# A state-space scan with an ELU layer on one core: block 0's and block 1's C loaded as squares by head pair, and the last four row pieces multiplied tile by tile

## The chip, the cores and the metric

The kernel runs on one core of one Trainium2 chip. The metric is device time in microseconds of one execution, lower is better. A core has a matrix engine (TensorE, PE in the profile, with its weight loads as PEld), a vector engine (VectorE, DVE), an engine for functions (ScalarE, ACT), a general engine (GpSimd, POOL) and one that here only issues transfers (SyncE, SP). Each works through its own queue in program order; semaphores join them. Transfers run on 16 DMA engines.

## The reference, cut to what matters

```python
# x: (4, 8, 768, 32), a: (4, 8, 768), B and C: (4, 8, 768, 16)
for c in range(24):                       # chunks of 32 tokens
    cum = cumsum(log(clip(a_c)))
    M = (C_c @ B_c.T) * exp(cum_i - cum_j) * causal
    y_c = M @ x_c + (C_c @ state) * exp(cum)
    state = exp(sum) * state + sum_j(B_j x_j * exp(cum_last - cum_j))
h = y.reshape(3072, 256) @ w_in           # heads side by side; w_in: 256 x 2048
g = where(h > 0, h, exp(min(h, 0)) - 1)
out = g @ w_out                           # w_out: 2048 x 256
```

The two weight matrices arrive as 64-bit floats; the kernel reads them as pairs of 32-bit words and makes float32 of them itself.

## The kernel before, in words

**Blocks.** The 3072 rows are worked on in 12 blocks of 256 tokens (`place`, L103, gives batch and group). Each block is first scanned, with inner chunks of 64 tokens, and its result, transposed, goes through the two weight matrices. There are no loops on the chip: the Python loops write out one long program, and the order in it is the order on each engine.

**The scan of a block.** B and C of a block lie in one tile `bc`, with tokens on the 128 partitions. `load_bc` (L121) loads B and C for both halves (`u`) of 128 tokens, in runs of 16 numbers, 64 bytes. For blocks from 4 on, and for C of block 1, `load_squares` (L111) loads the same data in another order, runs of 8 tokens by 16 numbers, so that 32 by 32 squares can be transposed by VectorE (`turn_square`, L454). The plain form is transposed by TensorE: `turn` (L430) transposes B and C, copies B from PSUM on ScalarE (`bt`) and makes on VectorE the C that is masked by head (`ctm`, L444); `turn_b` (L420) does B alone; `mask_heads` (L466) makes `ctm` from a square. `scaled` (L410) multiplies B by its decay, `turn_exp` (L448) multiplies C by the decay from the chunk's start (`cts`). Then `sums` (B times x), `states` (the running state, VectorE, and its masked copy, GpSimd), `scores` (C times B), `weigh` (L558, the scores times the decays, VectorE), `across` and `inside` (the carried and the inner part of y, TensorE), and copies into `yT`. For blocks 0 and 1 the decays come from a short first load of `a` (four loads of 32 rows, L93); `la` (L259) is the whole of `a`, clipped (L1118), turned into logarithms (L1154), and summed for all later blocks, whose sums go through memory (`write_flat`, `spread_cum`).

**The weights.** `w_load(i)` (L173) loads piece i of w_in (512 KB, piece 0 in two parts). Each piece is made into float32 by a fixed series: magnitude on ScalarE (`w_abs`, L201), low word on ScalarE or VectorE (`w_low`), sign and two steps on VectorE (`w_sign`, `w_high_a` L239, `w_high_b` L246), and the sum on GpSimd (`w_sum`, L256), for pieces 2 and 3 in two halves. Then `l1` (L678) multiplies.

**The start of the program.** All loads but two go out on SyncE's queue, in this order: two of the four `a` loads, B of block 0 (two halves), `la`, x of block 0 (two), piece 0 (two parts), piece 1, C of block 1 as two square loads, B's first half of block 1, piece 2, B's second half, piece 3, x of block 1 with piece 4 between its halves. ScalarE's queue carries the other two `a` loads and C of block 0 (two halves). The part that follows (from L1114) interleaves block 0's scan, pieces 0 to 3 and block 1's scan by hand; there `scaled(1)` (L1169, GpSimd) stands ahead of the sum of piece 2.

**The end of the program.** The last two blocks' second multiplication (`second_words`, L1029) is done in split words: each row piece m of 16 (`TURN`, L1009, the last 14 of them) has three products for each of the four tiles t of 128 rows: kind 1 into `both`, kinds 0 and 2 into `high[t]`. A loop does all products of a piece, four tiles by three kinds, and with them makes the words of the piece six places on (`high_of_g`, `rest_of_g` L1022). The last two pieces are done apart: first kind 1 for all tiles, whose result ScalarE scales into `e` (L1074), then kinds 0 and 2 tile by tile. After tile 1 VectorE combines tiles 0 and 1 (L1081), after tiles 2 and 3 each of those, and each tile is stored by a transfer of 128 KB, in turn on ScalarE's and SyncE's queue.

Of the kernel before, what the change touches and what calls it, by code (L numbers as in the profile page):

```python
# [32 lines left out]
def kernel(  # L33
# [69 lines left out]
    def place(n):  # L103

        return 2 * (n // (2 * NG)) + n % 2, n // 2 % NG
# [5 lines left out]
    def load_squares(n, k):  # L111
        b, g = place(n)
        squares = st[n]["bc"].rearrange("p k u h n -> p k (u h n)").rearrange(
            "p k (m r) -> p k m r", m=2)
        for m in range(2):
            nc.sync.dma_start(
                out=squares[:, k, m],
                in_=(B, C)[k][b, m:NH:2, g * BLK:(g + 1) * BLK, :].rearrange(
                    "q (c t) n -> q c (t n)", t=8))

    def load_bc(n, c_queue=nc.sync, us=(0, 1)):  # L121
        b, g = place(n)
        if "bc" not in st.setdefault(n, {}):
            st[n]["bc"] = raw.tile([P, 2, 2, NH, N], F32, tag="bc", name="bc", bufs=2)
        if n > 3:
            for k in range(2):
                load_squares(n, k)
            return
        for u in us:
            sl = slice((2 * g + u) * P, (2 * g + u + 1) * P)  # L130
            for k, src in enumerate((B,) if n == 1 else (B, C)):
                (nc.sync, c_queue)[k].dma_start(
                    out=st[n]["bc"][:, k, u], in_=src[b, :, sl, :].rearrange("h s n -> s h n"))

    def load_b(n):
# [37 lines left out]
    def w_load(i, parts=1):  # L173
        if i < len(pieces):
            w_raw[i] = conv.tile(
                [P, parts, 2, 2 * CW // parts], U32, tag="s64" if 5 <= i < 8 else "w64", name="w64",
                bufs=3 if 5 <= i < 8 else W_AHEAD - 3)
            for part in range(parts):
                cols = slice(2 * CW * part // parts, 2 * CW * (part + 1) // parts)
                nc.sync.dma_start(out=w_raw[i][:, part], in_=pieces[i][1][:, :, cols])  # L180
# [74 lines left out]
        w = pieces[i][0].bitcast(U32)[:, ks, cols]  # L255
        nc.gpsimd.tensor_tensor(out=w, in0=w_mag[i][:, ks, cols], in1=w, op=ALU.add)  # L256

    load_bc(0, nc.scalar)
    nc.sync.dma_start(out=la, in_=a.rearrange("b h (g c s) -> (b h g) c s", g=NG, s=P))  # L259
    load_x(0)  # L260
    w_load(0, 2)

# [167 lines left out]
    def turn(n):  # L430

        s = st[n]
        tb, tc_ = psum([P, 2, P], "ps_tb"), psum([P, 2, P], "ps_tc")
        for k, ps in enumerate((tb, tc_)):
            for u in range(2):
                nc.tensor.transpose(
                    out=ps[:, u], in_=s["bc"][:, k, u].rearrange("p h n -> p (h n)"),
                    identity=ident)
        s["squares"] = att.tile([P, 2, 2, P], F32, tag="bct", name="bct", bufs=2)
        s["bt"] = s["squares"][:, 0]  # L440
        nc.scalar.copy(out=s["bt"], in_=tb)
        s["ct"] = tc_
        s["ctm"] = att.tile([P, 2, 2, P], F32, tag="ctm", name="ctm")
        nc.vector.tensor_tensor(  # L444
            out=s["ctm"], in0=tc_.unsqueeze(2).to_broadcast([P, 2, 2, P]),
            in1=hmask2.unsqueeze(1).unsqueeze(3).to_broadcast([P, 2, 2, P]), op=ALU.mult)
# [19 lines left out]
    def mask_heads(n):  # L466
        s = st[n]
        s["ctm"] = att.tile([P, 2, 2, P], F32, tag="ctm", name="ctm")
        for us, eng in ((slice(0, 1), nc.vector), (slice(1, 2), nc.gpsimd)) if n == 1 else (
                (slice(0, 2), nc.vector),):  # L470
            count = us.stop - us.start
            eng.tensor_tensor(
                out=s["ctm"][:, us], in0=s["ct"][:, us].unsqueeze(2).to_broadcast([P, count, 2, P]),
                in1=hmask2.unsqueeze(1).unsqueeze(3).to_broadcast([P, count, 2, P]), op=ALU.mult)
# [354 lines left out]
    def row_of(n):  # L829
        b, g = place(n)  # L830
        return b * S + g * BLK
# [197 lines left out]
    def second_words(n):  # L1029

        both = [psum([P, 2, DM], "ps_w") for _ in range(2)]
        high = psum([P, 2, DM], "ps_o")
        high = [high[:, 0], high[:, 1], psum([P, DM], "ps_o"),
                p_o.tile([P, DM], F32, tag="o", name="ps_o")]

        def product(m, t, kind):
            lhs = h_of[m][kind][:, t // 2, t % 2 * P:(t % 2 + 1) * P]
            nc.tensor.matmul(  # L1038
                out=both[t // 2][:, t % 2] if kind == 1 else high[t], lhsT=lhs,
                rhs=out_words(m // 2, kind, m), start=(m == TURN[0] and kind == 0 and t != 1),  # L1040
                stop=(m == TURN[-1] and kind > 0), skip_group_check=True)

        store(n - 2, 0)
        store(n - 2, 1)
        given_back(slice(1, 4))
        for m in range(2):
            for t in range(4):
                nc.tensor.matmul(  # L1048
                    out=both[t // 2][:, t % 2], lhsT=g_of[n, m][:, t // 2, t % 2 * P:(t % 2 + 1) * P],
                    rhs=scaled_rows[0][:, m], start=(m == 0 and t % 2 == 0), stop=False,  # L1050
                    skip_group_check=True)
        rest_of_g(n, TURN[4])
        high_of_g(n, TURN[5])
        rest_of_g(n, TURN[5])
        for at, m in enumerate(TURN[:-2]):
            if at + 6 < len(TURN):
                high_of_g(n, TURN[at + 6])
            if at == 0:
                end_words()
            if at + 6 < len(TURN):  # L1060
                rest_of_g(n, TURN[at + 6])
            if at in (0, 2, 4):
                high_of_out(4 + at // 2)
            if at in (1, 3, 5):
                rest_of_out(4 + at // 2)
            for t in range(4):
                for kind in (1, 0, 2):
                    product(m, t, kind)
        e = [ffn.tile([P, 2, DM], F32, tag="e", name="e", bufs=2) for _ in range(2)]
        for b in range(2):  # L1070
            for t in (2 * b, 2 * b + 1):
                for m in TURN[-2:]:
                    product(m, t, 1)
            nc.scalar.activation(e[b], both[b], ACT.Copy, scale=WORD)  # L1074
        for t in range(4):
            for m in TURN[-2:]:
                product(m, t, 0)
                product(m, t, 2)
            for to in ((), (0, 1), (2,), (3,))[t]:
                o = e[to // 2][:, to % 2]  # L1080
                nc.vector.scalar_tensor_tensor(  # L1081
                    out=o, in0=high[to], scalar=WORD - 1.0, in1=o, op0=ALU.mult, op1=ALU.add)
                r0 = row_of(n + to // 2) + to % 2 * P
                (nc.scalar if to % 2 == 0 else nc.sync).dma_start(out=out[r0:r0 + P, :], in_=o)

    def store(n, at):
        r0 = row_of(n + at)
# [15 lines left out]


    w_load(1)
    load_bc(1, us=())
    load_squares(1, 1)
    load_bc(1, us=(0,))
    w_load(2)
    load_bc(1, us=(1,))  # L1110
    w_load(3)
    load_x(1, 4)
    half = [slice(0, P), slice(P, 2 * P)]
    first_low(0)  # L1114
    first_cum(0)
    first_decays(0, 0, 1)
    eb0 = turned(E0, "eb0", 1.0, nc.vector)
    clip(la)  # L1118
    turn(0)
    first_decays(0, 2)  # L1120
    first_exp(0)
    first_decays(0, 3)
    scaled(0, nc.gpsimd)
    turn_exp(0)
    sums(0, parts=(most,))
    states(0, most)
    w_abs(0, half[0])
# [17 lines left out]
    w_high_b(0, half[1])  # L1145
    kept = st[0]
    inside(y, 0)
    w_low(0, nc.scalar, half[1])
    w_sum(0, half[1])
    first_low(1, p_o)  # L1150
# [377 lines left out]
```

## Time and profile before

| what | value |
|---|---|
| time, median of 3 runs | 347.93 us (346.98 to 347.99) |
| profiled execution | 347.17 us, its span 345.5 us |
| TensorE busy | 337.1 us (98%), 3836 products |
| VectorE busy | 272.6 us (79%) |
| ScalarE busy | 250.1 us (72%) |
| GpSimd busy | 209.7 us (61%) |
| granted TensorE clock | 1.000 |
| TensorE idle, 15.95 to 27.23 us | 11.28 less 9.70 busy |
| TensorE idle, 27.23 to 341.00 us | 313.77 less 313.50 busy |
| DMA | 28.57 MB in 76645 packets, 57848 of them under 512 B |
| DMA engines busy, 5 to 25 us | nearly all the time, 221 to 262 GB/s |

The profile is of one execution. A line of a timeline gives the start in us from the start of the span, the length, the engine and the line of the code, the operation, what it writes and from what, and in brackets how long its engine stood idle before it and whom it waited for. A line with x2 or more merges instructions that follow one another. In the chain of waits each line is the piece of work that released the next; SPq and ACTq are the queues' own instructions, such as the issue of a transfer. "Busy" of TensorE says that it has products under way, not that it could do no more.

### The profile page before, as it was taken

What the parts mean: (1) busy time and instruction counts of PE and PEld (TensorE: products, weight loads), DVE (VectorE), ACT (ScalarE), POOL (GpSimd) and SP (SyncE); (2) the same over time, 40 slices, a digit from 0 to 9 for tenths busy, and PEclk for the clock granted to TensorE, in tenths of its full rate; (3) what the DMA queues carried; (4) which work ended last, traced back from release to release, by engine and by line L of the source; (5) the groups of instructions that cost most, each with busy time, mean ns of one, the idle gap of its engine ahead of it and who ended that gap; (6) DMA issues with size and microseconds to landing.
All of it is one profiled execution on the core that took longest, in us unless ns stands there. A gap on an engine that the chain in (4) does not pass through costs nothing.

```text
span 345.5 us, 9778 instructions
## 1 busy us (share of the span) xinstructions
PE 337.1 (98%) x3836; PEld 295.2 (85%) x3836; DVE 272.6 (79%) x527; ACT 250.1 (72%) x565; POOL 209.7 (61%) x303
## 2 busy tenths in 40 slices
PE   8889999999999999999999999999999999999994
PEld 5668888888788898889899888999988999999994
DVE  4898888879898778866788666879776778887991
ACT  5789889599759898657699457699557567768511
POOL 5754553559988799964396764296754562753600
PEclk9999999999999999999999999999999999999999
DMA  8988998380796961160421160510000100001001
GB/s 144 239 214 194 309 192 214 77 156 31 110 153 107 143 105 29 18 155 2 109 61 31 17 153 5 121 17 3 2 0 4 64 0 3 0 0 61 2 2 62
DMA packets 76645, 28.57 MB, mean 83 GB/s; under 512 B 57848, under 2 KB 71480, under 8 KB 76600
## 3 DMA queue, kind: packets, MB, share of 16 engines
q1 hardware_dynamic: 69960, 25.40, 32.1%
q0 software_dynamic: 4176, 2.10, 5.5%
q10 hardware_dynamic: 2464, 0.46, 0.7%
q8 instruction: 30, 0.49, 0.6%
q14 instruction: 15, 0.12, 0.1%
HBM read 22.51 MB, written 3.34 MB: 75 GB/s over the span
## 4 chain that ended last, share of the span: by engine, by line
PE 90%; DVE 3%; SPq 2%; DMA 2%; issue 1%; ACT 0%; DVEq 0%; ACTq 0%
PE ps_o L905 29%; PE ps_h L798 19%; PE ps_h L678 10%; PE ps_w L798 10%; PE ps_o L842 8%; PE ps_o L1038 4%; PE ps_y L645 2%; PE ps_w L1038 2%; DMA w<-in_moe_w_in_dram 2%; PE ps_g L552 2%; PE ps_y L627 1%; PE ps_st L582 1%; PE ps_w L1048 1%; SPq L180 1%; DVE g L700 1%
## 5 line engine op out<-in xcount | busy, mean ns | idle before, releaser
L815 ACT ACTIVATE e<-ps_h 128x512 f32<-128x512 f32 x72 | 43.1, 598 | 48.2 <-DVE ps_h L809 48.1
L823 DVE SCALAR_TENSOR_TENSOR g<-e,ps_h 128x512 f32<-128x512 f32 x72 | 49.3, 684 | 29.4 <-ACT e L816 29.0
L905 PEld LDWEIGHTS ps_o<-w_out,g 128*128 128x128 f32 x512 | 64.0, 191 | 3.4
L905 PE MATMUL ps_o<-w_out,g 128*128 128x128 f32 x512 | 65.3, 275 | 0.0
L809 DVE SCALAR_TENSOR_TENSOR ps_h<-ps_h,e 128x512 f32<-128x512 f32 x72 | 50.0, 694 | 11.5 <-ACT e L806 10.7
L798 PE MATMUL ps_w<-y_both,w_words 128*128 128x512 f32 x144 | 51.1, 435 | 0.0
L806 ACT ACTIVATE e<-ps_w 128x512 f32<-128x512 f32 x72 | 42.1, 584 | 10.8 <-PE ps_w L798 10.7
L678 PE MATMUL ps_h<-yT,w_in 128*128 128x256 f32 (+1 forms) x208 | 45.4, 368 | 2.5 <-POOL w_in L256 0.6
L816 ACT ACTIVATE e<-e 128x512 f32<-128x512 f32 x72 | 45.5, 632 | 2.3
L798 PE MATMUL ps_h<-y,w_words 128*128 128x512 f32 x144 | 46.0, 401 | 0.0
L798 PE MATMUL ps_h<-y,w 128*128 128x512 f32 x144 | 44.7, 392 | 0.0
L858 POOL TENSOR_TENSOR g<-g 128x256 f32<-128x256 f32 x28 | 22.2, 794 | 36.4 <-DVE g L823 36.2
L678 PEld LDWEIGHTS ps_h<-yT,w_in 128*128 128x128 f32 x208 | 36.2, 190 | 8.5 <-POOL w_in L256 3.4
L532 ACT ACTIVATE L<-L,ncum 128x64 f32<-128x64 f32 x160 | 42.2, 336 | 0.4 <-DVE ncum L377 0.4
L537 POOL TENSOR_SCALAR_AFFINE_SELECT L<-L 64x512 f32<-64x512 f32 x40 | 30.0, 750 | 9.0 <-ACT L L532 7.6
L798 PEld LDWEIGHTS ps_h<-y,w 128*128 128x128 f32 x144 | 27.0, 188 | 6.5 <-POOL w L858 0.2
L905 PE MATMUL ps_o<-w_sum,g 128*128 128x128 f32 x256 | 32.6, 275 | 0.0
L905 PEld LDWEIGHTS ps_o<-w_sum,g 128*128 128x128 f32 x256 | 31.4, 192 | 1.3 <-ACT c_sum L942 0.3
L798 PEld LDWEIGHTS ps_h<-y,w_words 128*128 128x128 f32 x144 | 26.4, 188 | 5.7 <-issue 0.4
L842 PE MATMUL ps_o<-w_out,g 128*128 128x256 f32 x128 | 31.0, 384 | 0.0
L842 PEld LDWEIGHTS ps_o<-w_out,g 128*128 128x128 f32 x128 | 23.7, 190 | 4.0 <-ACT ob L848 0.4
L858 POOL TENSOR_TENSOR g<-t,g 128x256 f32<-128x256 f32 x32 | 23.0, 747 | 5.8 <-PE ps_o L905 5.7
(144 smaller groups left out, 636.9 us busy)
## 6 DMA issues: line engine op xcount, KB each, us to landing
L<-flat SPq DMA_DIRECT2D x20, 256.0 KB
w<-in_moe_w_out_dram SPq DMA_DIRECT2D x8, 512.0 KB
w<-in_moe_w_in_dram SPq DMA_DIRECT2D x7, 512.0 KB
xr<-in_x_dram SPq DMA_DIRECT2D x24, 128.0 KB
out_dram<-c_sum SPq DMA_DIRECT2D x8, 256.0 KB
bc<-in_B_dram SPq DMA_DIRECT2D x24, 64.0 KB
w_sum<-w_out POOLq DMA_DIRECT2D x3, 512.0 KB, 8.9
bc<-in_C_dram SPq DMA_DIRECT2D x22, 64.0 KB
```

Source lines behind the costliest of these rows:

```text
L532: nc.scalar.activation(L[:, h, u], L[:, h, u], ACT.Exp, bias=ncum[:, u, row:row + 1])
L537: nc.gpsimd.affine_select(out=part, in_=part, pattern=[[0, 4], [0, 2], [1, Q]], compare_op=ALU.is_ge, fill=0.0, base=0, channel_multiplier=-1)
L678: nc.tensor.matmul(out=ps[:, j, toks], lhsT=w_in[i][:, k, j * P:(j + 1) * P], rhs=yT[n // 2][:, k, n % 2].rearrange("p u i -> p (u i)")[:, ...
L798: nc.tensor.matmul(out=ps, lhsT=lhs[:, k], rhs=rhs[:, k], start=k == 0 and lhs is not w0, stop=k == KC - 1 and lhs is not w1)
L806: nc.scalar.activation(e, both, ACT.Copy, scale=WORD)
L809: nc.vector.scalar_tensor_tensor(out=high, in0=high, scalar=WORD - 1.0, in1=e, op0=ALU.mult, op1=ALU.add)
L815: nc.scalar.activation(e, high, ACT.Relu, scale=-1.0)
L816: nc.scalar.activation(e, e, ACT.Exp, scale=-1.0)
L823: nc.vector.scalar_tensor_tensor(out=g_of[n, m].rearrange("p b i -> p (b i)"), in0=e, scalar=1.0, in1=h, op0=ALU.subtract, op1=ALU.max)
L842: nc.tensor.matmul(out=o_of[n][:, ts], lhsT=g_of[n, j][:, m % 2, ts * P:(ts + 1) * P], rhs=w_out[:, m], start=(m == 0 and ts == 0), stop=( ...
L858: nc.gpsimd.tensor_tensor(out=out, in0=in0, in1=in1, op=ALU.subtract)
L905: nc.tensor.matmul(out=ps[:, ts], lhsT=b[:, ts * P:(ts + 1) * P], rhs=a[:, i], start=(i == chunk[0] and ts == 0), stop=(i == chunk[-1]), s ...
```

## The change

Block 0's C is no longer loaded by `load_bc` in 64-byte runs, but as squares by the new `load_c_square`: one transfer for each pair of heads q, 32 partitions of the tile, in runs of 512 bytes, quarters 0 and 3 on ScalarE's queue, 1 and 2 on SyncE's, with B's two halves among them. Block 1's C is loaded by four such transfers in place of two of 128 rows. The load of `la` moves from ahead of x of block 0 to behind piece 1; piece 2 moves ahead of block 1's C, and B's two halves of block 1 lie on either side of piece 3.

In the scan of block 0 the C square is transposed by VectorE, and `ctm` made half on VectorE and half on GpSimd, as block 1 has it; TensorE transposes B alone; `scaled(0)` goes from GpSimd to VectorE and `turn_exp(0)` from VectorE to GpSimd. The clip of `la` moves behind block 0's `inside`.

At the end four row pieces are done apart, not two: kind 1 for all four pieces and two tiles, then the other two tiles; then kinds 0 and 2 tile by tile. Tiles 0 and 1 are combined and stored by one transfer after tile 1, tile 2 after tile 2, and tile 3 in two halves of 128 columns, each stored by itself.

```diff
+    def load_c_square(n, q, queue=nc.sync):
+
+        b, g = place(n)
+        queue.dma_start(
+            out=st[n]["bc"][32 * q:32 * q + 32, 1].rearrange("p u h n -> p (u h n)").rearrange(
+                "p (m r) -> p m r", m=2),
+            in_=C[b, 2 * q:2 * q + 2, g * BLK:(g + 1) * BLK, :].rearrange(
+                "m (c t) n -> c m (t n)", t=8))
...
-            for k, src in enumerate((B,) if n == 1 else (B, C)):
-                (nc.sync, c_queue)[k].dma_start(
+            for k, src in enumerate((B,) if n < 2 else (B, C)):
+                nc.sync.dma_start(
...
-    load_bc(0, nc.scalar)
-    nc.sync.dma_start(out=la, in_=a.rearrange("b h (g c s) -> (b h g) c s", g=NG, s=P))
+    load_bc(0, (0,))
+    load_c_square(0, 0, nc.scalar)
+    load_c_square(0, 1)
+    load_bc(0, (1,))
+    load_c_square(0, 2)
+    load_c_square(0, 3, nc.scalar)
     load_x(0)
     w_load(0, 2)
...
-        for us, eng in ((slice(0, 1), nc.vector), (slice(1, 2), nc.gpsimd)) if n == 1 else (
+        for us, eng in ((slice(0, 1), nc.vector), (slice(1, 2), nc.gpsimd)) if n < 2 else (
...
-        for at, m in enumerate(TURN[:-2]):
+        for at, m in enumerate(TURN[:-4]):
...
         for b in range(2):
-            for t in (2 * b, 2 * b + 1):
-                for m in TURN[-2:]:
+            for m in TURN[-4:]:
+                for t in (2 * b, 2 * b + 1):
                     product(m, t, 1)
             nc.scalar.activation(e[b], both[b], ACT.Copy, scale=WORD)
+
+        def end(t, cols=slice(0, DM)):
+            o = e[t // 2][:, t % 2, cols]
+            nc.vector.scalar_tensor_tensor(
+                out=o, in0=high[t][:, cols], scalar=WORD - 1.0, in1=o, op0=ALU.mult, op1=ALU.add)
+            return o
+
+        r0 = row_of(n + 1)
         for t in range(4):
-            for m in TURN[-2:]:
+            for m in TURN[-4:]:
                 product(m, t, 0)
                 product(m, t, 2)
-            for to in ((), (0, 1), (2,), (3,))[t]:
...
+            if t == 1:
+                end(0)
+                end(1)
+                to = row_of(n)
+                nc.scalar.dma_start(
+                    out=out[to:to + BLK, :].rearrange("(t p) e -> p t e", p=P), in_=e[0])
+            if t == 2:
+                nc.sync.dma_start(out=out[r0:r0 + P, :], in_=end(2))
+            if t == 3:
+                for cols, queue in zip(half, (nc.scalar, nc.sync)):
+                    queue.dma_start(out=out[r0 + P:r0 + BLK, cols], in_=end(3, cols))
...
     w_load(1)
+    nc.sync.dma_start(out=la, in_=a.rearrange("b h (g c s) -> (b h g) c s", g=NG, s=P))
+    w_load(2)
     load_bc(1, us=())
-    load_squares(1, 1)
+    for q in range(4):
+        load_c_square(1, q)
     load_bc(1, us=(0,))
-    w_load(2)
+    w_load(3)
     load_bc(1, us=(1,))
-    w_load(3)
     load_x(1, 4)
...
+    turn_square(0, 1)
+    mask_heads(0)
     eb0 = turned(E0, "eb0", 1.0, nc.vector)
-    clip(la)
-    turn(0)
-    first_decays(0, 2)
+    turn_b(0)
     first_exp(0)
-    first_decays(0, 3)
-    scaled(0, nc.gpsimd)
-    turn_exp(0)
+    first_decays(0, 2, 3)
+    scaled(0, nc.vector)
+    turn_exp(0, nc.gpsimd)
...
     inside(y, 0)
+    clip(la)
     w_low(0, nc.scalar, half[1])
```

More of the change, by code (lines that the diff above doesn't have):

```diff
@@ L119, in load_squares, with load_bc @@
                     "q (c t) n -> q c (t n)", t=8))
-    def load_bc(n, c_queue=nc.sync, us=(0, 1)):
+    def load_c_square(n, q, queue=nc.sync):
[5 more added lines that the diff above has]
+                "m (c t) n -> c m (t n)", t=8))
+    def load_bc(n, us=(0, 1)):
         b, g = place(n)
@@ L1070, in second_words @@
         for b in range(2):
-            for t in (2 * b, 2 * b + 1):
-                for m in TURN[-2:]:
+            for m in TURN[-4:]:
+                for t in (2 * b, 2 * b + 1):
                     product(m, t, 1)
             nc.scalar.activation(e[b], both[b], ACT.Copy, scale=WORD)
+        def end(t, cols=slice(0, DM)):
[4 more added lines that the diff above has]
+        r0 = row_of(n + 1)
         for t in range(4):
-            for m in TURN[-2:]:
+            for m in TURN[-4:]:
                 product(m, t, 0)
                 product(m, t, 2)
-            for to in ((), (0, 1), (2,), (3,))[t]:
[L1080 to L1084, printed above, removed]
+            if t == 1:
[9 more added lines that the diff above has]
+                    queue.dma_start(out=out[r0 + P:r0 + BLK, cols], in_=end(3, cols))
     def store(n, at):
```

## The prediction

> **What bounds the kernel now.** The page first: TensorE carries nine tenths of the chain that ended last.
>
> ```profile
> PE 337.1 (98%) x3836; PEld 295.2 (85%) x3836; DVE 272.6 (79%) x527; ACT 250.1 (72%) x565; POOL 209.7 (61%) x303
> ...
> PE 90%; DVE 3%; SPq 2%; DMA 2%; issue 1%; ACT 0%; DVEq 0%; ACTq 0%
> ```
>
> So I ask from when TensorE has no gap. The chain in order of time, cut to 0 to 40 us (start, length, what), answers that:
>
> ```profile
> 8.79 0.47 SPq L132
> ...
> 9.30 5.96 DMA w<-in_moe_w_in_dram
> ...
> 15.35 0.64 ACT ps_mag L201
> ...
> 16.02 0.70 DVE ps_mag L239
> 16.72 0.74 DVE sgn L228
> ...
> 27.23 5.34 PE ps_h L678 x38
> ```
>
> Read downwards: SyncE issues one load after another until 9.30; the load of w_in piece 2 lands at 15.27; ScalarE takes its magnitude; VectorE then runs without a gap from 16.02 to 27.2; from 27.23 TensorE is fed to the end (the longest other piece in the chain after that is 0.12 us). What makes TensorE gapless sooner therefore moves the end by as much, and what happens on other engines after 27.23 moves nothing as long as it stays on time. Two places are left where time can be won: before 27.23, and after the last product (340.95).
>
> VectorE's timeline for the early part (start, length, operation, in brackets its idle time before and who ended it):
>
> ```profile
> 7.12 0.69 DVE L444 TENSOR_TENSOR ctm<-ps_tc,hmask 128x512 f32<-128x512 f32 x1
> ...
> 9.08 1.41 DVE L561 TENSOR_TENSOR M<-ps_g,L 128x256 f32<-128x256 f32 x4
> ...
> 12.92 0.70 DVE L239 TENSOR_SCALAR ps_mag<-ps_mag 128x512 f32<-128x512 f32 x1 [0.24 <-ACT ps_mag L201]
> ...
> 16.02 0.70 DVE L239 TENSOR_SCALAR ps_mag<-ps_mag 128x512 f32<-128x512 f32 x1 [1.08 <-ACT ps_mag L201]
> ...
> 19.68 0.83 DVE L472 TENSOR_TENSOR ctm<-bct,hmask 128x256 f32<-128x256 f32 x1
> ```
>
> From block 0's weighing (9.08) on, VectorE idles only twice, 0.24 and 1.08 us, both behind ScalarE's magnitude, which waits for w_in pieces 1 and 2. Why they are late is in the DMA view for 7.4 to 13.5 us (40 slices; tenths busy, then GB/s):
>
> ```profile
> DMA  8999999997569975977699557896555325976999
> GB/s 248 316 376 349 316 403 376 410 289 188 107 175 215 228 255 228 363 271 266 224 300 335 183 160 154 162 181 116 107 87 93 68 50 83 231 195 242 332 354 300
> ```
>
> The rate falls from 400 to 50 GB/s while work is queued. In this stretch lie the two square loads of block 1's C; the completion events of the trace for them run from 8.5 to 13.5 us, 64 KB each, after only four of the usual sixteen engines' worth of events. The engines that carry them hold up pieces 1 and 2 (landed 12.15 and 15.27).
>
> The Trainium skill, "DMA: Bandwidth & Descriptors", section "Why a DMA increments its semaphore by 16 and not by 1", says a transfer is spread over the largest number up to 16 that divides the slowest dimension of both sides. Here these are 128 and 4, so four engines: the trace agrees. In the new form they are 32 and 32.
>
> **The start, part by part.** *C of block 0.* Gone: two loads of 1024 packets of 64 B on ScalarE's queue. The DMA view for 1.5 to 8.6 us gives that queue 2176 packets and 23.6% of 16 engines, 1.68 us of all engines, C having 2048 of the packets: about 1.6 us. Added: four quarters of 32 KB in 512 B packets. Nearest row: the four loads of `a`, also 32 rows of 32 KB, end 0.17 to 0.39 us apart while issue paces them, so at most 0.2 us each, 0.8 in all; at least what 32 KB take at 340 GB/s, 0.1 each. Net 0.8 to 1.2 us of DMA time saved ahead of everything.
>
> *Ahead of piece 2* also go the block 1 C squares and B's first half (the stretch of 50 GB/s), and `la` (96 KB) goes behind piece 1. SyncE issues one DMA fewer before piece 2 (12th, not 13th), at 0.40 to 0.58 us each when not held back: 6.5 to 7 us instead of 9.30. The 512 KB of a piece land 1.68 us after the piece before (the completions of pieces 7 and 8). So piece 1 lands at 9.5 to 10.5 and piece 2 at 11.2 to 12.5; even with piece 1 no earlier than now, piece 2 comes at 13.8. Piece 3 follows at 13.5 to 16; its ScalarE step is due at about 17. B's second half, now behind piece 3, lands by 14 to 16.8; GpSimd's `scaled(1)`, queued ahead of the sum of piece 2, is due at 16.4: nothing to 0.4 us of wait.
>
> *Block 0 up to the weighing.* VectorE between 5.54 and 9.08 loses the clip of `la` (0.29), the masked C (0.69) and the scaled C (0.42). It gains the transposition of the square (0.65 in the row of block 1), one half of the mask, and `scaled(0)`, 128x256, 0.42 like the L452 row of that size. The mask half took 0.83 in block 1 beside GpSimd's half of 0.75; without such company 0.42. The transposition fits into the 0.96 us in which VectorE now waits (5.54 to 6.50) if C's last quarter has landed. It is queued behind B's second half on SyncE; B's halves now land at 4.80 and 6.08 with C between them, so without C about 4.6 and 5.3, and the quarter by 5.5. Then: square 5.55, mask 6.15, `eb0` 6.6 to 7.0, `scaled(0)` 6.85 to 7.25, sums 0.45 later, scores (0.73) behind them, weighing 0.1 after that: 8.7 to 9.2, against 9.08. I take 9.05. The scaled C moves to GpSimd (0.72 like `scaled` there) behind ScalarE's `ec` (7.6): ready at 8.35, needed by the carried part at 9.5: hidden by 1.1 us. TensorE's two C transposes go; it was not the limit there.
>
> The Trainium skill, "SBUF — State Buffer", section "Who interferes with whom", has a rule against this: a VectorE operation with two SBUF inputs and a GpSimd operation lock each other out, the later one standing still. The two mask rows agree with it; by the rule the weighing would be at 9.2, the upper end above.
>
> *From the weighing on* the clip (0.29, issued 0.27 apart) comes into VectorE's stream near 12.2; the two idle times (1.32) go, since pieces 1 and 2 are there by about 11.8 and 13.5, when ScalarE is free. Sum at 16.02: 0.03 + 1.32 - 0.27 = 1.08 earlier (bounds: -0.12 and +0.38 for the weighing, so 0.9 to 1.45; less 0.4 if GpSimd waits for B: 0.5). Is the next limit nearer? GpSimd: sum of piece 1 14.4 to 15.9, then `rest_of_sums` and `scaled(1)` (0.61 each), sum of piece 2 at 17.05 instead of 18.05: 1.0. TensorE: from 16.06 to 27.23 its idle time is 1.54 us (11.28 less 9.70 busy, nearly the same), and it can start that stretch 0.1 earlier: at most 1.65. So GpSimd and VectorE come out alike, and I take **1.05 us**.
>
> **The end.** The timeline of VectorE (its last word splits, then the last four results) and of SyncE's queue (its last two stores):
>
> ```profile
> 333.72 2.48 DVE L1025 SCALAR_TENSOR_TENSOR g_words<-g_words,g 128x512 fp32r<-128x512 f32 x4
> 340.10 1.42 DVE L1081 SCALAR_TENSOR_TENSOR e<-ps_o,e 128x256 f32<-128x256 f32 x4 [3.89 <-PE ps_o L1038]
> ...
> 340.93 1.34 SPq L1084 DMA_DIRECT2D out_dram<-e  x2
> ```
>
> Products stay 48, 0.12 us each, so TensorE's end stays at 340.95 relative to its start. Now four VectorE operations begin after tile 1 (two thirds through the last 16 products), spaced 0.33 us: the last starts at 341.11, ends 341.52; its store is issued at 341.92, lands 343.91, and 1.55 us of closing follow. After: tiles 0 and 1 are ready two tiles (1.92 us) earlier and tile 2 one (0.96), so the last tile finds VectorE free at 341.06. Halves of 128 columns take 0.28 (0.69 for 512 columns and 0.415 for 256 give 0.14 per 128) and start 0.19 apart: ends 341.34 and 341.53. The second half is thus no earlier than now; what is saved is data: 64 KB less behind it, 0.19 us at 340 GB/s, and the 0.2 us by which the last store took longer than the first (1.98 against 1.77). SyncE's issue came 0.37 us after its tile; whether that goes is open. Gain 0 to 0.75, I take 0.35. Against it: "both" words of the last row piece are now used at 335.63 (weights of the seventh product of the 48 from 335.03), not 338; VectorE has them at 335.61, so a stall of 0 to 0.1: I take 0.05. Net **0.30 us**.
>
> **Sum:** 1.05 + 0.30 = 1.35. The profiled execution took 347.17 (span 345.5 and 1.7 around it) and would take 345.8; the runs' median of 347.93 lies 0.76 above it, and I forecast for that median 346.6. A measurement of this kernel tells 0.3% (1.04 us) from no change.
>
> **Rivals.** *Hidden start.* Pieces land sooner, but GpSimd's wait for B's second half (0.4), weighing at 9.2 and a tail that gives nothing leave 1.45 - 0.38 - 0.12 - 0.4 = 0.55: 347.4. For it: all three sit on queues in order; against: they need not come together. *TensorE bound.* All 1.65 and a tail of 0.65: 2.3, so 345.6. Against: VectorE's stream alone allows 1.45. *Slower.* C's last quarter lands late. From the transposition to the weighing it is 0.6 + 0.5 + 0.25 + 0.42 + 0.45 + 0.83 = 3.05 us in one line, so weighing slips once the quarter lands after 6.0, and the whole gain of 1.35 is gone at 7.4, 0.9 later than C lands now (6.52); at 8.0 the time is 348.5. For it: four small transfers instead of two, one behind B's 64 B packets. Against: less is queued ahead of it than now.
>
> The Trainium skill, "SBUF — State Buffer", section "Door 1: The DMA port swizzle", gives 32 rows half of the ports, as few as 64 rows. By it a quarter takes twice 0.1 us, the upper price above; C would land some 0.4 later, at 5.9, still before 6.0. The loads of `a` do not contradict it.
>
> **Chances.** Forecast (0.9 to 1.9 gained) 0.55; TensorE bound 0.10; hidden start (0 to 0.9) 0.27; slower rival 0.08. Faster by over 0.3%: nine tenths of the first and all of the second, 0.60. Slower by over 0.3%: half of the last and some drift, 0.06. Within: 0.34. Range: from the TensorE bound less 0.2 (345.4) to a gain of 0.3 (347.6).
>
> **What would show it.** Right: no idle before VectorE's step on piece 2; that step at about 14.9; C squares of block 1 complete within 1 us; TensorE gapless by 26.2; the last product to the end 4.2 us instead of 4.5. Wrong: GpSimd idle ahead of `scaled(1)`; weighing after 9.3; a gap in TensorE's last 48 products; a new DMA wait of ScalarE after 27.

## The result and the profile after

The changed kernel takes 346.39 us (median of 17 runs, 345.27 to 347.82), the kernel before in the same session 347.29 us (17 runs): a ratio of 0.9969, 95% interval 0.9957 to 0.998. The forecast was 346.6. The profiled execution took 346.39 with a span of 344.7, before 347.17 with 345.5. The time came out near the forecast; the two parts of the gain did not, as the views show.

The page after: TensorE's busy time and the shares of the chain that ended last.

```profile
PE 337.1 (98%) x3834; PEld 295.1 (86%) x3834; DVE 273.2 (79%) x529; ACT 250.2 (73%) x565; POOL 210.7 (61%) x304
...
PE 92%; DMA 3%; SPq 2%; DVE 1%; POOL 0%; issue 0%; DVEq 0%; POOLq 0%
```

The chain in order of time, cut to 0 to 40 us (start, length, what):

```profile
11.87 0.38 SPq L189
...
12.30 5.04 DMA bc<-in_B_dram
...
17.48 0.62 POOL sc L429
18.10 0.90 POOL w_in L265
...
27.15 5.34 PE ps_h L691 x38
```

VectorE's idle time behind pieces 1 and 2 has left the chain. In its place stands a load: B's second half of block 1, issued at 12.30 and landed at 17.34, for which GpSimd's `scaled(1)` (L429) waits, with the sum of piece 2 (L265) queued behind it. TensorE is gapless from 27.15, before from 27.23: of the 1.05 us forecast for the start, this execution shows 0.08. Over the next 20 us it loses more, 0.19 us of idle time ahead of block 2's sums (42.57 us) and a little in block 2's part of y, and the last product starts at 340.88, before at 340.67.

The wait itself, on GpSimd's timeline:

```profile
17.48 0.62 POOL L429 TENSOR_TENSOR sc<-bc,eb 128x256 f32<-128x256 f32 x1 [0.82 <-DMA bc<-in_B_dram]
18.06 1.79 POOL L265 TENSOR_TENSOR w_in<-mag,w_in 128x256 uint32<-128x256 uint32 x2
```

VectorE's timeline shows where the step was right, and what came behind it:

```profile
9.11 1.41 DVE L574 TENSOR_TENSOR M<-ps_g,L 128x256 f32<-128x256 f32 x4
...
14.75 0.67 DVE L248 TENSOR_SCALAR ps_mag<-ps_mag 128x512 f32<-128x512 f32 x1
...
19.19 0.95 DVE L248 TENSOR_SCALAR mag<-mag 128x512 f32<-128x512 f32 x1
20.17 1.05 DVE L255 SCALAR_TENSOR_TENSOR mag<-mag,sgn 128x256 uint32<-128x256 uint32 x2
```

Weighing at 9.11 and the step on piece 2 at 14.75 (before 16.02), both without an idle bracket. But at 19.19 and 20.17 VectorE's steps on piece 3 take 0.95 and 1.05 us. In the trace of before the same two took 0.42 and 0.76, in a pause of GpSimd (20.23 to 21.45):

```profile
20.43 0.42 DVE L239 TENSOR_SCALAR mag<-mag 128x512 f32<-128x512 f32 x1
20.88 0.76 DVE L246 SCALAR_TENSOR_TENSOR mag<-mag,sgn 128x256 uint32<-128x256 uint32 x2
```

Now they lie beside GpSimd's late sum of piece 2 (18.06 to 19.85, 1.79 us, before 1.42) and its mask. Of the lead of 1.27 us at 14.75, 0.42 is left when they end (21.22, before 21.64).

The DMA view for 7.4 to 13.5 us, the same stretch as in the prediction (40 slices; tenths busy, then GB/s):

```profile
DMA  9998889965979798999999999999999999858899
GB/s 322 329 309 289 282 282 208 208 228 222 302 295 322 309 363 342 343 376 376 336 369 390 390 396 322 309 349 376 316 309 308 236 175 305 121 109 192 210 159 259
```

The stretch at 50 to 100 GB/s is gone: the four quarters of block 1's C no longer hold it up. The pieces did not gain as much. Piece 1 landed at 11.86 (before 12.15), piece 2 at 13.74 (15.27), piece 3 at 17.06 (18.11); B's second half landed at 17.34 (15.63). All C quarters of block 1 now land between 14.92 and 15.77. SyncE stands from 10.29 to 11.87: by the semaphores in the trace its transfers share eight completion semaphores in turn, and the issue of piece 3 begins at 11.87, 0.02 us after piece 1, eight transfers back, has landed. In the same way that of x (13.76) comes right behind the landing of piece 2 (13.74). So the queue in front of piece 3 got shorter in bytes, and longer in transfers.

The end: VectorE's last results, and then SyncE's last two stores.

```profile
339.70 1.09 DVE L1091 SCALAR_TENSOR_TENSOR e<-ps_o,e 128x256 f32<-128x256 f32 x3 [3.29 <-PE ps_o L1051]
341.19 0.49 DVE L1091 SCALAR_TENSOR_TENSOR e<-ps_o,e 128x128 f32<-128x128 f32 x2 [0.41 <-PE ps_o L1051]
```

```profile
340.81 0.35 SPq L1107 DMA_DIRECT2D out_dram<-e  x1
341.71 0.35 SPq L1110 DMA_DIRECT2D out_dram<-e  x1
```

VectorE is free at the last tile (idle 0.41) and the last store goes out 0.03 us after its half is ready; before it went out 0.40 us after. From the start of the last product to the end of the span it is 3.78 us, before 4.79: 1.01 us less, more than the whole difference of the two spans. The profile thus puts the gain at the end and none at the start. The experiments test that.

### The profile page after: what moved, and what is told of

Same layout as the page of the kernel before. It is cut to its first block, busy times and chain, and to the rows that moved or that the text cites. A ratio compares the mean times of both kernels' runs of the same rounds, so it can differ in the third digit from the quotient of the medians.

```text
span 344.7 us, 9784 instructions
## 1 busy us (share of the span) xinstructions
PE 337.1 (98%) x3834; PEld 295.1 (86%) x3834; DVE 273.2 (79%) x529; ACT 250.2 (73%) x565; POOL 210.7 (61%) x304
## 4 chain that ended last, share of the span: by engine, by line
PE 92%; DMA 3%; SPq 2%; DVE 1%; POOL 0%; issue 0%; DVEq 0%; POOLq 0%
PE ps_o L918 29%; PE ps_h L811 19%; PE ps_h L691 11%; PE ps_w L811 10%; PE ps_o L855 8%; PE ps_o L1051 4%; PE ps_y L658 2%; PE ps_w L1051 2%; PE ps_g L565 2%; DMA w<-in_moe_w_in_dram 2%; DMA bc<-in_B_dram 1%; PE ps_y L640 1%; PE ps_st L595 1%; PE ps_w L1061 1%; SPq L189 0%; DVE M L574 0%
## 5 line engine op out<-in xcount | busy, mean ns | idle before, releaser
L822 DVE SCALAR_TENSOR_TENSOR ps_h<-ps_h,e 128x512 f32<-128x512 f32 x72 | 50.0, 694 | 11.2 <-ACT e L819 10.0
L819 ACT ACTIVATE e<-ps_w 128x512 f32<-128x512 f32 x72 | 42.0, 584 | 11.2 <-PE ps_w L811 11.1
```

Of the source, the lines that this page charges most:

```text
L819: nc.scalar.activation(e, both, ACT.Copy, scale=WORD)
L822: nc.vector.scalar_tensor_tensor(out=high, in0=high, scalar=WORD - 1.0, in1=e, op0=ALU.mult, op1=ALU.add)
```

## The experiments

For each, the ratio is to the kernel before on the same chip, with its 95% interval, and the difference is that of the medians. The runs come from three sessions on three chips, so across sessions ratios are compared, not times. One outlying execution moves the ratio more than it moves the difference of the medians.

**The end alone.** The kernel before with the end of the changed one:

```diff
...
-            for t in (2 * b, 2 * b + 1):
-                for m in TURN[-2:]:
+            for m in TURN[-4:]:
+                for t in (2 * b, 2 * b + 1):
...
+            if t == 3:
+                for cols, queue in zip(half, (nc.scalar, nc.sync)):
+                    queue.dma_start(out=out[r0 + P:r0 + BLK, cols], in_=end(3, cols))
...
```

> The kernel before with the new end alone. Theory 1 (the prediction's split): the end is worth 0.3 us, so about 0.3 faster than before, and 3.9 to 4.4 us from the last product to the end of the span. Theory 2 (read from the profile after, where that stretch is 3.5 us against 4.5 before): the end is worth 0.8 to 1.0 us, nearly the whole gain, and the stretch is 3.5 us again.

Measured: 346.84 against 347.36 (-0.52), ratio 0.9984, 0.9973 to 0.9995. From the start of the last product to the end 4.22 us, against 4.79. By the ratio the end alone gives half of the change's gain, between the two theories.

**The start alone.** The changed kernel with the old end:

```diff
...
-            for m in TURN[-4:]:
-                for t in (2 * b, 2 * b + 1):
+            for t in (2 * b, 2 * b + 1):
+                for m in TURN[-2:]:
...
```

> The changed kernel with the old end: the new start alone. Theory 1: 1.05 us faster than before. Theory 2: 0 to 0.3 us faster, since GpSimd's scaling of block 1's B waits for B's second half, which lands at about 17.3 us, and stands ahead of the sum of piece 2; TensorE is gapless from 27.1 us, as before.

Measured: 347.42 (+0.06), ratio 0.9997, 0.9977 to 1.0017: the start alone gives nothing that can be told, and it scatters more (345.77 to 349.77). In its profiled execution another wait is the late one: piece 1 lands at 12.88 and `la`, queued behind it, at 13.10, and VectorE's clip of `la`, in order ahead of the work on piece 1, waits 0.77 us for it. TensorE is gapless only from 28.02.

**B of block 1 sooner.** If B's second half is the wait, loading it earlier should help. Both halves go ahead of block 1's C and of piece 3:

```diff
-    load_bc(1, us=())
+    load_bc(1, us=(0, 1))
     for q in range(4):
         load_c_square(1, q)
-    load_bc(1, us=(0,))
     w_load(3)
-    load_bc(1, us=(1,))
```

> The changed kernel with both halves of block 1's B ahead of its C and of piece 3. Theory 2 (the wait for B's second half took the start's gain): B's second half lands by about 15.5, GpSimd's wait of 0.82 us is gone, TensorE is gapless by about 26.4 and the kernel 0.4 to 0.8 us faster than the changed one. Rival (the wait only fills time that VectorE, slowed beside GpSimd, needs anyway): no faster than the changed kernel within 0.2.

Measured: 348.60 (+1.24), ratio 1.0036, 1.0015 to 1.0057, slower. SyncE's queue shows one reason:

```profile
9.06 6.17 SPq L124 DMA_DIRECT2D bc<-in_C_dram  x4
```

B's second half did land sooner, at 14.67, and GpSimd no longer waits for it. But behind B's 2048 packets of 64 B the four C issues take 6.17 us, 4.76 of them the first one; in the changed kernel they take 2.12. All that follows is late: piece 3 is issued at 15.27, not 11.87, x of block 1 has landed in full only at 22.9, and TensorE's sums of block 1 wait 0.70 us for it. The late load can be swapped for another late load. The late loads are not all of the loss: six of the twelve executions have a mean granted clock of 0.995 or less and took 348.46 to 350.26, the five at 1.000 took 346.82 to 348.08 (see the last section).

**GpSimd's wait taken out.** `scaled(1)` goes behind both halves of piece 2's sum:

```diff
-    scaled(1, nc.gpsimd)
     for cols in half:
         w_high_b(2, cols)
         w_sum(2, cols)
+    scaled(1, nc.gpsimd)
```

> The changed kernel with GpSimd's scaling of block 1's B behind both halves of the sum of piece 2, the loads as they are. Theory 2: the sum of piece 2 begins at about 16.8 in place of 18.1, TensorE's products on piece 2 at about 18.5 in place of 19.0, and the kernel is 0.3 to 0.8 us faster than the changed one. Rival (the scaling, now late, holds up block 1's sums, or VectorE is the bound): within 0.2 of the changed kernel.

Measured: 346.31 (-1.05), ratio 0.9965, 0.9952 to 0.9979, the same as the changed kernel. The wait is gone and the sum of piece 2 starts at 17.29, before at 18.05, but TensorE is gapless only from 26.86 and the last product starts at 340.80, 0.13 us later than before. Taking out the wait that stood in the chain was worth nothing that can be told. By this profile the next things to arrive stand right behind it: VectorE's step on piece 3 beside GpSimd takes 0.83 us, and TensorE waits 0.65 us for block 1's state; no run took these out.

**Block 0's C on one queue.** All four quarters on ScalarE's queue, which leaves SyncE's to B, x and the pieces:

```diff
-    load_c_square(0, 0, nc.scalar)
-    load_c_square(0, 1)
+    for q in range(4):
+        load_c_square(0, q, nc.scalar)
     load_bc(0, (1,))
-    load_c_square(0, 2)
-    load_c_square(0, 3, nc.scalar)
```

> The changed kernel with all four C quarters of block 0 on ScalarE's queue, so that SyncE has two issues fewer ahead of x, of pieces 0 and 1 and of a's whole load. Theory 3 (up to 8 us the loads come at the pace of SyncE's issues, 0.45 to 0.58 us each, not at that of the packets): piece 1 and a's whole load land 0.5 to 0.9 us earlier than in the changed kernel (11.9 and 12.2 us) and the kernel is 0.3 to 0.8 us faster than it. Rival (the DMA engines set the pace, SyncE only queues ahead of them): piece 1 lands within 0.3 of 11.9 and the time is within 0.2.

Measured: 347.31 against 347.01 (+0.30), ratio 1.0021, 1.0009 to 1.0034, slower. Piece 1 was issued at 6.12, sooner than in the changed kernel, and landed at 11.97, no sooner: in this stretch the pace of the DMA engines sets when it lands, not the issue. And ScalarE's own work stood behind the issues (its first step on `a` at 4.73, in the changed kernel at 3.86): C's last quarter landed at 7.46 and block 0's weighing came at 11.27. That is the slower rival of the prediction, which had the gain gone with C at 7.4; from the square's transposition to the weighing it is 3.62 us here and 3.41 in the changed kernel, where the prediction had 3.05.

**Block 1's C in two transfers again**, to give SyncE two completion semaphores back:

```diff
-    for q in range(4):
-        load_c_square(1, q)
+    load_squares(1, 1)
```

> The changed kernel with C of block 1 loaded by the two transfers of 128 rows that the kernel before has, so two transfers fewer. Theory 4 (SyncE's issue of piece 3 stands until piece 1 has landed because at most eight transfers may be under way): piece 3 is issued at about 10 us in place of 11.9 and B's second half lands before 16.5. Prediction's reason (two transfers on four engines hold up the pieces): piece 2 lands later than 13.7 by 0.5 to 1.5 us and the kernel is slower than the changed one by up to 0.5.

Measured: 346.85 (-0.16), ratio 1.0002, 0.9988 to 1.0016. Piece 3's issue started at 9.64, before piece 1 had landed, but took 3.37 us; piece 2 landed at 13.78, as in the changed kernel (13.74), B's second half at 16.9 instead of 17.34. So the eight semaphores are one brake; with it off, the issue itself took longer, for a reason the trace doesn't show, and the bytes arrived at nearly the same pace. The prediction's reason doesn't show either: queued behind piece 2, two transfers on four engines do not make it later. Yet the ratio is above the changed kernel's 0.9969, and the intervals don't meet. The place of the last store (third, not fifth; explained below) accounts for 0.12 us of that; the rest is open.

**Both.** All quarters of block 0's C on ScalarE's queue and `scaled(1)` behind the sum, the diffs of those two runs together:

> Both edits together: all C quarters of block 0 on ScalarE's queue, and GpSimd's scaling of block 1's B behind the sum of piece 2. Theory 3 with theory 2: TensorE is gapless by 26.2 us and the kernel is 0.6 to 1.0 us faster than the changed one. Rival: as the changed kernel within 0.3.

Measured: 348.02 (+1.01), ratio 1.0036, 1.0022 to 1.0049. No gain from the two together, but the run says little of the two theories. In its profile C's last quarter landed at 6.81, sooner than with C on one queue alone, and yet the weighing came at 11.86. TensorE was busy without a gap from 6.01 to past it, and its products took up to twice as long. The scores, here and then in the changed kernel:

```profile
10.46 1.38 PE L563 MATMUL ps_g<-ctm,bct 32*64 32x128 f32 x32
```

```profile
8.08 0.69 PE L565 MATMUL ps_g<-ctm,bct 32*64 32x128 f32 x32
```

The trace's records of the granted clock begin at 13.97 us in this execution, in the changed kernel's at 4.38 (see the last section).

**Four transfers more.** The end's 1.01 us in the trace is more than what the end alone gave (0.57 there). The rest would have to come from something at the end that the new end's own edit does not hold. At the close SyncE waits for the eight completion semaphores in a fixed order, one wait each 0.06 us (343.92, 343.98, 344.04, ... 344.34 in the trace of before). Before, the last store is on the first of the eight, so all other waits come behind it; the changed kernel issues four loads more, and its last store is on the fifth. Four stores in the middle of the kernel before, split in two, move its last store to the fifth too:

```diff
+        for t in range(2) if n < 6 else ():
+            nc.sync.dma_start(
+                out=out[r0 + t * P:r0 + (t + 1) * P, :],
+                in_=c_of[n][:, at, t].rearrange("p e c -> p (e c)"))
+        if n < 6:
+            return
```

> The kernel before with four stores of the middle split in two, so four transfers more and nothing else; the last store then ends on another of the eight semaphores on which the program's last waits stand. Theory 5 (after the last store the program goes through eight waits in a fixed order, 0.06 us each, and the changed kernel's count of transfers alone moves the last store from the first to the fifth of them): 0.2 to 0.5 us faster than before. Theory 1 (only bytes and products count at the end): no change within 0.1.

Measured: 346.48 (-0.53), ratio 0.9991, 0.998 to 1.0002: at the edge, so by itself inconclusive. In its profile the last product to the end is 4.10 us, 0.69 less than before, with the old stores.

**The end and four transfers more**, with the old start, so the diff of the end alone and this last one:

> The kernel before with the new end (as in the run of the end alone, which gained 0.52 us) and four transfers more in the middle (as in the run of four more alone, which gained 0.53 us, with an interval that just takes in no gain); the start is the old one. Theory, that the start of the changed kernel is worth nothing and that the rest of its gain comes from the place of the last store's semaphore among the eight closing waits (fifth, not first: four waits of 0.062 us fewer behind it, 0.25 us, and up to 0.5): 0.75 to 1.0 us less than before, as the changed kernel; from the last store's landing to the end 1.1 us, not 1.34. Rival, that the place is worth nothing and the start gives the other half: 0.5 us less than before, as the end alone.

Measured: 346.15 against 346.94 (-0.79), ratio 0.9977, 0.9969 to 0.9986. That agrees with the changed kernel's 0.9969 (0.9957 to 0.998), without its start. The closing took 1.09 us from the last landing, as in the changed kernel, and not 1.34 as with the end alone.

**The place moved in the changed kernel.** The same split of four stores puts the last one back on the first semaphore, of three on the eighth:

> The changed kernel with four stores in the middle split in two, four transfers more, so that the last store's semaphore is again the first of the eight that are waited for at the close. Theory of the place: 0.25 us or somewhat more is lost against the changed kernel, so 0.5 to 0.8 us less than the kernel before; from the last landing to the end 1.35 us, not 1.09. Rival, that the place is worth nothing: 1.0 us less than before, as the changed kernel.

> The changed kernel with three stores in the middle split in two, three transfers more, so that the last store's semaphore is the last of the eight that are waited for at the close. Theory of the place: three waits of 0.062 us fewer behind the last landing than in the changed kernel, 0.19 us gained: 1.15 to 1.25 us less than before, and 0.9 us from the last landing to the end. Rival, that the place is worth nothing: 1.0 us less than before, and the same close.

Measured: with four 346.62 (-0.32), ratio 1.0003, 0.998 to 1.0025; with three 346.13 (-0.81), ratio 0.9973, 0.9963 to 0.9984. The times alone don't settle it, since the first scattered from 345.81 to 350.54 and the second gained no more than the changed kernel, where 1.15 to 1.25 us had been expected; the closings in the profiles do: 1.34, 1.09 and 0.90 us on the first, fifth and eighth place, 0.06 us for each place. Block 1's C in two transfers fits in between, with 1.21 us on the third.

**Four pieces apart, old stores.** The order of the products as changed, with one store of 128 KB for each tile as before:

```diff
-        for at, m in enumerate(TURN[:-2]):
+        for at, m in enumerate(TURN[:-4]):
...
-            for m in TURN[-2:]:
+            for m in TURN[-4:]:
```

> The kernel before with four row pieces done apart, tile by tile, but each tile combined and stored as before (one transfer of 128 KB a tile). Theory of the prediction: VectorE is free at the last tile, so its last result starts some 0.17 us sooner than before, but it takes 0.42 us for 256 columns and the last store carries 128 KB: 0.1 to 0.2 us less than before, against 0.5 for the whole new end. Rival, that the new end gains by the tile order alone and the halves of the last tile are worth nothing: 0.5 us less than before. The number of transfers is that of before, so the place of the last semaphore is the same.

Measured: 347.11 (+0.17), ratio 1.0008, 1.0 to 1.0017: the order of the products alone gives nothing, where theory and rival both had a gain. In its profile VectorE is done 0.74 us after the start of the last product (before 0.85), but TensorE's last 48 products took 5.95 us, before 5.64: the row piece whose words are now used sooner was waited for, 0.31 us.

The end of these kernels, in us from the start of the last product, from the trace:

| kernel | VectorE done | last store issued | landed | end | place of its semaphore |
|---|---|---|---|---|---|
| before | 0.85 | 1.25 | 3.23 | 4.79 | first |
| four pieces, old stores | 0.74 | 1.13 | 2.99 | 4.56 | first |
| four transfers more | 0.85 | 0.91 | 2.79 | 4.10 | fifth |
| end alone | 0.80 | 0.83 | 2.88 | 4.22 | first |
| end and four more | 0.81 | 0.83 | 2.82 | 3.92 | fifth |
| after | 0.80 | 0.83 | 2.69 | 3.78 | fifth |
| after and four more | 0.81 | 0.83 | 2.68 | 4.02 | first |
| after and three more | 0.81 | 0.84 | 2.53 | 3.44 | eighth |

Read by columns: halves of the last tile do not end VectorE's work much sooner (0.80 against 0.85) nor shorten the last store (1.69 to 2.05 us from issue to landing in the five kernels with halves, against 1.86 to 1.98 in the three with the old stores). What goes is a pause of SyncE between its wait for the tile and the store, 0.40 us before and 0.39 with four pieces and old stores, 0.03 to 0.07 in all others; and in the closing of 1.56 us a VectorE drain that came 0.2 us late, which the three with the old stores have and none with the new. The start alone, with the old stores too and its last store on the fifth place, has neither: its store goes out 0.06 us after VectorE is done and its closing takes 1.08 us. With four transfers more the pause went though the stores stayed as they were. Why these two come and go is open.

## Why the prediction was right, and where it was not

The time was right, at 0.2 us, but in part by luck. The forecast of 346.6 was a gain of 1.35 us from a median of 347.93; in the session of the result the kernel before took 347.29, 0.64 less, and the gain was 0.90. And the split of the gain into start and end was wrong: an end worth more than forecast stood in for a start worth nothing.

*Start, 1.05 us: mis-sized, measured about nothing.* With the same end and the same closing, the new start has ratio 0.9969 and the old one 0.9977, and their intervals overlap. The two other pairs that differ by the start alone say the same: with the old end and the last store on the fifth place 0.9997 (new start) and 0.9991, with the new end and the first place 1.0003 and 0.9984. In the five profiles with the old start the last product starts at 340.12 to 340.84, in the nine with the new one at 340.80 to 344.81. On VectorE the terms held up to its step on piece 2: C ahead of its use (landed 5.67, forecast 5.5; transposition 5.70, forecast 5.55), weighing 9.11 (9.05), the clip moved in, two idle times out, step on piece 2 at 14.75 (14.9). The landings did not: pieces 1, 2 and 3 came at 11.86, 13.74 and 17.06, forecast 9.5 to 10.5, 11.2 to 12.5 and 13.5 to 16. The step on piece 2 was right because the prediction had also allowed for piece 2 at 13.8. The step that failed is the one after it, "GpSimd and VectorE come out alike". GpSimd waited 0.82 us for B's second half where 0 to 0.4 was allowed: I had it landing by 14 to 16.8, with SyncE issuing without a break; its issue stood behind that of piece 3, which was held by the eight transfers under way, and it landed at 17.34. The hidden start was a rival in the forecast, with its chance at 0.27 and GpSimd's wait as its mechanism. But taking that wait out gave nothing, so it was only the first of several. That the bytes come at the pace of the DMA engines, and that whichever load is put last ends the chain, is read from the landings in four runs with the loads in another order, form or queue; no run had fewer bytes to load.

The Trainium skill, "SBUF — State Buffer", section "Who interferes with whom", has VectorE and GpSimd lock each other out when VectorE's operation has two SBUF inputs, as the step of 1.05 us has, or runs in a two-port mode, which the section lists for a `tensor_scalar` like that of 0.95 us; the prediction weighed the rule for one mask alone. The two rows above (0.95 and 1.05 us beside GpSimd, 0.42 and 0.76 in its pause) agree with it, and they took back part of the lead in a place where I had not looked for it.

*End, 0.30 us: mis-sized, measured 0.5 for the end alone and 0.8 with four transfers more.* "Last product to the end 4.2 us instead of 4.5", counted from the product's end, came out as 3.5. The term for data (0.39) was far too large: the last store lands 1.86 us after its issue, before 1.98, and in the four other kernels with halves it takes 1.69 to 2.05. SyncE's 0.37 us behind the tile, left open in the prediction, did go, and the closing shrank by 0.47: 0.25 for four waits fewer behind the last landing, 0.22 for the late drain. The place of a store's semaphore is set by the number of transfers in the whole program, so the quarter loads of the start, four more than the loads they replace, paid at the end. No term of the sum had that.

*Stall, 0.05.* In the profiled execution 0.01 (5.65 against 5.64 us for the last 48 products), but 0.3 in three of eleven profiled executions with this order. So it comes in some executions and not in others; a small constant was the wrong form. With one profile for each kernel it is open whether it is chance.

*TensorE gapless by 26.2:* wrong, 27.15. *C squares of block 1 within 1 us:* right, 0.85. *No new wait of ScalarE after 27:* wrong, there are two, behind pieces of w_in (0.54 us at 33.53, 0.56 at 38.03; before none), but TensorE has no gap there. *TensorE bound* fell with the start. *C late* did not occur (5.67); with all quarters on ScalarE's queue it did, and the gain was gone as worked out (C at 7.46).

## What to carry to other kernels

An idle time taken out of one engine pays only up to the next thing that lands late; where the loads run at the DMA engines' full pace, ask which load is last after the change, and what stands in order behind it, before adding up the idle times. Count a change's transfers, not only its bytes: they take completion semaphores, queue places and the order of the closing waits, and here a count that shifts by four moved the closing by 0.25 us, over a quarter of the whole gain. Split a result by the trace (last product to end, start to gapless) before believing that the sum was right for its reasons.

## What the runs showed of the hardware that was not expected

**TensorE stood where its code came late.** The profile's page lists a queue q8 "instruction" with 30 packets and 0.49 MB. With 7668 of the 9784 instructions TensorE's (products and weight loads), that much code is TensorE's. The packet records have the first of these blocks within the span start at 10.1 to 11.1 us in all five kernels with the old start, and at 10.8 to 14.3 in the nine with the new one, in the stretch of the DMA view above. In three of these, TensorE stood at the same product, one without any wait on a semaphore, until 1.32 to 1.42 us after that packet had ended: the changed kernel (packet until 13.76, product at 15.08), with three transfers more (14.07, 15.41) and with four more (15.38, 16.80). That the packet is what it stood for is read from these times; no run took it away, and that the loads made it late is argued from where it lies. The Trainium skill, "Runtime: NRT & Kernel Launch", section "Instruction fetch mechanics", has code refilled by a DMA queue of the engine's own in blocks of 16 KiB, mostly hidden; the packets have that size, and here it was not hidden.

**The granted clock can fall to half after a short gap.** The changed kernel with four transfers more, TensorE's timeline:

```profile
13.73 1.13 PE L691 MATMUL ps_h<-yT,w_in 128*128 128x256 f32 x4 [0.23 <-POOL w_in L265]
16.80 1.16 PE L516 MATMUL ps_x<-first,ident 32*64 32x128 f32 x32 [1.94 <-issue]
17.89 1.24 PE L524 MATMUL ps_x<-minus,first 32*128 32x128 f32 x16
19.06 3.78 PE L691 MATMUL ps_h<-yT,w_in 128*128 128x256 f32 x8
```

and its windows (busy time of each engine, the granted clock, DMA share, GB/s):

```profile
14.00:16.00 2.00, 0.86 (x4) 0.41 (x3) 1.97 (x4) 1.98 (x5) 0.36 (x1) 1.00 0.98 280
16.00:18.00 2.00, 1.20 (x36) 0.87 (x36) 1.97 (x5) 1.17 (x3) 1.91 (x2) 0.66 0.63 96
18.00:20.00 2.00, 2.00 (x18) 1.67 (x19) 2.00 (x5) 0.85 (x4) 1.30 (x2) 0.50 0.68 221
```

TensorE stands 1.94 us, the granted clock is 0.50 from 16.65 to 23.48, and eight products take 3.78 us where they took 1.99: the last product starts 3.9 us later than in the changed kernel. The length of the gap is not the whole rule. With three transfers more a gap of 1.22 us left the clock at 1.00. With B first the clock is 0.50 from 28.51 to 31.92, where the longest waits of TensorE in the 10 us before were 1.04 us (until 21.25) and 0.70 us (until 22.91). What sets the fall off is open. Executions with a mean clock of 0.995 or less were 11 of 103 with the new start (six of them in the run with B first, one of 17 in the changed kernel), none of 143 with the old one (the record has no clock for the 17 of the kernel before in the session of the result). So part of the new start's scatter upward is this; not all, since with C on one queue three executions took 348.4 to 348.5 at a clock of 1.000. The Trainium skill, "TensorE: Matmul & The Clock Gate", section "Why this matters for your kernels", warns of gaps over some 3 us; here the clock fell in one of 1.94 us, and in another run without a gap that long.

**TensorE's slow phase at the start ends at another time in each execution.** The trace's records of the granted clock begin between 4.06 us (the start alone) and 13.97 us (both edits), and up to there the products of a kernel take longer, as the two rows of scores above show (the windows view prints 1.00 where there is no record). In the five profiles with the old start block 0's weighing moves with it: at 9.08, 9.45, 9.61, 9.82 and 10.22 us with records from 4.56, 5.61, 5.92, 6.46 and 7.29. The mean clocks counted above don't hold this phase. With the old start it did not carry to the end: the last product of the second of these five starts sooner (340.12) than that of the first (340.67).
